# One query copy on ScalarE in place of GpSimd, and the low parts of the weights in two halves

## The chip, the cores and the metric

The kernel runs on one core of a Trainium2 chip. The metric is the device time of one execution in microseconds (us). The core has five engines, each with its own queue of instructions that it takes in order: TensorE (PE, with its weight loads as PEld), VectorE (DVE), ScalarE (ACT), GpSimd (POOL) and SyncE (SP), which issues most of the DMAs. An engine waits on semaphores for what other engines and DMAs have done.

## The reference

Two things are computed one after the other. First an attention over 8 batches, 8 heads, 576 positions and 64 values per head, in which a query sees only a window of keys: the last 32 for heads 0 to 3, every fourth of the last 128 for heads 4 to 7.

```
scores = scale * np.matmul(q, k.transpose(0, 1, 3, 2))
scores = np.where(masks, scores, -1e9)
attn = softmax(scores)
x = np.matmul(attn, v)        # then heads side by side: x is 8 x 576 x 512
```

Then in each batch the 128 rows with the highest score `x @ w_gate` go through two matrices (512x1024 and 1024x512) with a ReLU between them, and are added back, weighted with the sigmoid of their score:

```
scores = np.einsum('bsd,d->bs', x, w_gate)
top_idx = np.argpartition(-scores[b], capacity)[:capacity]
h = np.maximum(x[b, top_idx] @ w1, 0.0)
out[b, top_idx] = x[b, top_idx] + g[:, None] * (h @ w2)
```

## The kernel before, in words

The order of all work is written out by hand in one text, ORDER (lines 44 to 112). Each entry names a step and its batch, and a loop at the end of the kernel calls the step's function; since every engine takes its instructions in order, this text sets the order on each engine. The steps that matter here, as `NAME batch part`:

- Q and K load transposed queries and keys with SyncE's DMAs (lines 290 to 303). For each batch there are two kinds of heads (kind 0: the plain window, kind 1: every fourth key).
- ZP, ZV and ZA are the same function, `spread` (line 306): it copies one half of the loaded queries (64 partitions, h = 0 or 1) into a padded tile `zq` whose other places hold zeros. ZP does so on GpSimd, ZV on VectorE, ZA on ScalarE. There is one `zq` tile for each kind, so it is written anew in every batch once the last scores that read it are done.
- S (line 352 on) makes the scores of one of five groups of a batch: two matmuls with the masks, then 24 or 32 small matmuls of `kq` and `zq` into a PSUM tile `s` (line 363). There are two `s` tiles.
- MX takes the maxima on VectorE (line 370). Then either CS copies the scores to SBUF on ScalarE (line 377) and SP2 subtracts the maxima on GpSimd (line 382), or SU subtracts on VectorE. TR transposes the differences (line 389), EX takes the exponentials on ScalarE (lines 398 and 402), V multiplies with the values (line 417), DN and XM divide on VectorE (lines 426 to 438), ST stores the rows to HBM with SyncE's DMAs (lines 448 to 456).
- GD multiplies the rows with the gate and sums them, two instructions of VectorE with two inputs in SBUF, `x` and `wg` (line 474; the tile `warm` takes the product, which nobody needs). RX/RP, RO, SC, SP and RK make scores and ranks out of the sums (`gs`, then `ts`), and W fills TensorE's time with matmuls that read `warm` (line 712).
- GT gathers the chosen rows with an indirect DMA of GpSimd (line 597), XT transposes them (line 632), XH and XL split them into a high and a low part (lines 635 and 638). F and N are the first matrix (lines 653 and 669), Y is the second (line 694), YO the sum (line 699), SY the indirect store back (line 704), again from GpSimd.

The two matrices are held as a high part in a rounded format and a low part, what is left. LW loads one of eight blocks of 128x1024 as `raw` (lines 605 and 607; there are two `raw` tiles), WH rounds it on ScalarE (line 617), WL subtracts on GpSimd (line 621). The blocks are loaded and split between the attention steps of batches 0 to 4, and each product is then three matmuls: high by high, high by low, low by high.

Around the change in ORDER (lines 74 to 76) stand, in this order: GT 2 and SY 0 on GpSimd; ZV 4 0 0 on VectorE; CS 3 2 on ScalarE; the copy of the other half, ZP 4 0 1; the scores S 4 4 and S 4 3, the first to read `zq` of batch 4; EX 4 0, XH 1 and EX 3 3 on ScalarE; SP2 3 2 on GpSimd; then TR 3 2, XT 2, V 3 3 and S 4 2 on TensorE, and the first matrix of the next group (F 1 ..).

Of the kernel before, what the change touches and what calls it, by code (L numbers as in the profile page):

```python
# [8 lines left out]
F32 = mybir.dt.float32  # L9
# [4 lines left out]
ALU = mybir.AluOpType  # L14
# [3 lines left out]
B, H, S, D = 8, 8, 576, 64  # L18
DM, FF = 512, 1024
# [52 lines left out]
GD 2 2, SC 2, SP 2, ST 2 3, MX 3 4, V 3 0, VL 3 1, SU 3 4, ZP 4 1 0, ST 2 4, GT 1, RK 2 0, EX 3 1, RK 2 1, RK 2 2,  # L72
RK 2 3, TP 2, Q 4 0, S 4 1, RK 2 4, S 4 0, SP2 3 3, TR 3 3, WH 7, DN 3 0, K 4 0, MX 4 1, WL 7, RC 2, RA 2, TR 3 4,
MV 2, Y 0 6, CS 4 1, SP2 4 1, Y 0 7, MX 4 0, XA 3 0, PK 2, S 3 2, IX 2, GT 2, V 3 1, DT 4 0, SU 4 0, YO 0, Q 5 0,
TR 4 0, TR 4 1, DN 3 1, EX 3 4, XM 3 1, SY 0, ZV 4 0 0, XT 1, V 3 4, MX 3 2, DN 3 4, CS 3 2, ZP 4 0 1, S 4 4, S 4 3,
XM 3 4, EX 4 0, VL 5 2, XH 1, SP2 3 2, EX 3 3, TR 3 2, XT 2, ST 3 4, XL 1, V 3 3, CS 4 4, MX 4 4, XH 2, S 4 2, XL 2,
F 1 1 0, F 1 0 0, F 1 1 1, F 1 0 1, GM 3 0, GA 3 0, DT 4 3, MX 4 3, SU 4 3, F 1 0 2, SP2 4 4, GD 3 4, SG 2, DN 3 3,
EX 3 2, F 1 2 0, SG 1, F 1 1 2, F 1 1 3, GD 3 1, ST 3 1, RX 3, SH 1, ST 3 0, MX 4 2, XM 3 3, ZP 5 0 1, EX 4 1,
# [37 lines left out]
def tile_window_attention_moe(ctx, tc, qt, kt, va, vb, w_gate, w1, w2, masks, mask_l, ident, slots, toks, outs, capacity):  # L116
    nc = tc.nc
# [55 lines left out]
    X = {}  # L173
# [132 lines left out]
    def spread(copy, b, kind, h, part=None):  # L306
        r, src = slice(HB * h, HB * (h + 1)), qs[b, kind]
        n = 16 if kind else 18
        lo, hi = (0, n) if part is None else (0, 8) if part == 0 else (8, n)
        copy(zqs[kind][r, :, lo:hi, h], src[r, :, G * lo:G * hi].rearrange("p g (t q) -> p g t q", q=G))  # L310
        if hi == n:
            if kind:
                copy(zqs[kind][r, :, n:n + 4, h, 0:16], src[r, :, 4 * P:S].rearrange("p g (t q) -> p g t q", q=16))
            over(("q", b, kind), src, 2)
# [64 lines left out]
    def subtract(eng, b, u):  # L379
        st, mx = X.pop(("s", b, u)), X.pop(("mx", b, u))  # L380
        dt = X["dt", b, u]
        eng.tensor_tensor(out=dt, in0=st if eng is nc.vector else dt, in1=mx.unsqueeze(2).to_broadcast([P, 8, GK]), op=ALU.subtract)  # L382
# [46 lines left out]
    def divide(b, u, on_act):  # L429
        av, rin = heads(X.pop(("a", b, u))), X.pop(("rin", b, u))  # L430
        X["x", b, u] = x = xs.pop(0)
        xv = x.rearrange("p e (i d) -> p e i d", i=4)
        if on_act:
            for e in range(2):
                for i in range(4):
                    nc.scalar.activation(xv[:, e, i], av[:, e, i, 0:D], AF.Copy, scale=rin[:, e, i:i + 1])
        else:
            nc.vector.tensor_tensor(out=xv, in0=av[:, :, :, 0:D], in1=rin.unsqueeze(3).to_broadcast([P, 2, 4, D]), op=ALU.mult)  # L438
# [171 lines left out]
    def weight_parts(i):  # L610
        if i < 4:
            return (w[:, i] for w in (w1h, w1l))
        return (w[:, 2 * i - 8:2 * i - 6].rearrange("k j f -> k (j f)") for w in (w2h, w2l))
# [4 lines left out]

    def weights_low(i):
        hi, lo = weight_parts(i)  # L620
        nc.gpsimd.tensor_tensor(out=lo, in0=X.pop(("raw", i)), in1=hi.bitcast(F32), op=ALU.subtract)

    TERMS = (("h", "h", 0), ("h", "l", 1), ("l", "h", 2))
    WS1, WS2 = dict(h=w1h, l=w1l), dict(h=w2h, l=w2l)
# [83 lines left out]
    def idle(n):  # L708
# [8 lines left out]
        ZA=lambda *i: spread(nc.scalar.copy, *i), VL=load_v, C=constants, W=idle, S=scores, MX=maximum, SU=lambda *i: subtract(nc.vector, *i), DT=differences, CS=copy_scores, SP2=lambda *i: subtract(nc.gpsimd, *i), TR=turn, EX=exps,  # L717
        V=attend, DN=divisors, XM=lambda b, u: divide(b, u, False), XA=lambda b, u: divide(b, u, True), ST=store,
        GM=gate_mult, GA=lambda b, u: gate_sum(b, u, False), GD=lambda b, u: gate_sum(b, u, True),
        RX=lambda b: split_sums(nc.vector, b), RP=lambda b: split_sums(nc.gpsimd, b), TP=score_parts, RO=in_order, SC=total_score, SP=as_row, RK=rank, RC=rank_others, RA=rank_total,  # L720
        MK=lambda b: mark(b, 0, nc.gpsimd), MV=lambda b: mark(b, 0, nc.vector), PK=pick, IX=index, SG=sig_exp, SH=sig,
        GT=gather, LW=load_weights, WH=lambda i: weights_high(i, nc.scalar.copy), WV=lambda i: weights_high(i, nc.vector.tensor_copy),
        WL=weights_low, YO=result, SY=scatter)
    groups = {}
    for name in ORDER.split("\n"):
# [120 lines left out]
```

## Time and profile before

| what | us |
|---|---|
| median of 3 runs | 263.73 |
| lowest and highest of them | 262.48, 264.22 |
| the profiled execution | 263.13 |
| its span in the trace | 261.4 |
| TensorE busy in the span | 233.8 |
| VectorE, GpSimd, ScalarE busy | 183.2, 127.2, 121.0 |

The rows further down come from the one profiled execution, with times counted from the start of its span. A row of a timeline has the start, the duration, the engine, the line of the kernel, the operation, what is written and read, and how many instructions of it are merged; in brackets the time that the engine stood idle before it and what ended that. A name such as `zq L310` is the tile and the line of the instruction that wrote it. A granted clock of 1.00 is 2.4 GHz, one of 0.50 is 1.2 GHz.

### The profile page before, as it was taken

How to read it: one execution, taken by the hardware profiler on the slowest of the kernel's cores; microseconds unless marked ns; L12 is line 12 of the kernel's file. 1: busy time of each engine (PE TensorE's matmuls, PEld its weight loads, DVE VectorE, ACT ScalarE, POOL GpSimd, SP SyncE). 2: the span in 40 equal slices, each digit the busy share in tenths (PEclk: the TensorE clock that was granted, in tenths of full speed). 3: DMA queues.
4: the chain of work that ended last, by engine and by line, in shares of the span. 5: the costliest groups of instructions: out<-in, count | busy, mean ns of one | idle time of the engine just before them, and what ended most of it. 6: DMA issues, size and time to landing. Idle time of an engine off the chain costs nothing.

```text
span 261.4 us, 8703 instructions
## 1 busy us (share of the span) xinstructions
PE 233.8 (89%) x3560; PEld 205.1 (78%) x3560; DVE 183.2 (70%) x540; ACT 121.0 (46%) x265; POOL 127.2 (49%) x192
## 2 busy tenths in 40 slices
PE   5897689976998893899999988999999999999991
PEld 3785588875896682799888977999898888988880
DVE  6676998869789985185678687787878688831231
ACT  5278457693468445161613455863560443101120
POOL 6199769778578743612413658331427434110111
PEclk9799979997999998599999999999999999999999
DMA  6999797969749597907593753499258322201102
GB/s 239 391 374 326 219 380 252 330 203 332 299 146 337 180 332 233 286 4 234 206 301 143 239 181 112 115 289 386 98 146 290 97 80 95 94 0 40 43 0 80
DMA packets 22712, 53.14 MB, mean 203 GB/s; under 512 B 2816, under 2 KB 13440, under 8 KB 21648
## 3 DMA queue, kind: packets, MB, share of 16 engines
q1 hardware_dynamic: 20496, 47.63, 53.5%
q0 software_dynamic: 1344, 4.26, 5.0%
q10 hardware_dynamic: 832, 0.69, 0.8%
q8 instruction: 28, 0.46, 0.7%
q14 instruction: 12, 0.10, 0.1%
HBM read 41.04 MB, written 11.53 MB: 201 GB/s over the span
## 4 chain that ended last, share of the span: by engine, by line
PE 66%; DVE 18%; DMA 5%; ACT 4%; POOL 3%; issue 3%; POOLq 1%; SPq 0%; DVEq 0%; ACTq 0%
PE m L653 14%; PE m L694 14%; PE a L417 11%; PE s L363 10%; DVE warm L474 7%; PE m L669 5%; PE m L389 4%; PE s L356 3%; DVE x L438 2%; ACT pt L402 2%; DVE mx L370 2%; PE m L523 2%; DMA mraw<-in_masks_dram 2%; DMA out_dram<-x 1%; DMA out_dram<-y,ix 1%
## 5 line engine op out<-in xcount | busy, mean ns | idle before, releaser
L363 PEld LDWEIGHTS s<-kq,zq 128*64 128x64 f32 x1216 | 45.4, 148 | 9.9 <-POOL zq L310 5.8
L363 PE MATMUL s<-kq,zq 128*64 128x64 f32 (+2 forms) x1216 | 46.0, 232 | 6.1 <-POOL zq L310 5.2
L417 PE MATMUL a<-v,pt 128*64 128x65 f32 x1152 | 46.5, 226 | 3.5 <-DVE x L438 3.3
L417 PEld LDWEIGHTS a<-v,pt 128*64 128x64 f32 x1152 | 41.7, 140 | 8.4 <-issue 3.4
L382 POOL TENSOR_TENSOR dt<-dt,mx 128x512 f32<-128x512 f32 x28 | 29.9, 1070 | 33.6 <-DVE mx L370 19.1
L474 DVE CUSTOM_DVE_ANT_0 warm<-x,wg 128x256 bf16<-128x256 f32 x68 | 41.5, 610 | 4.3 <-PE m L712 2.6
L377 ACT COPY dt<-s 128x512 f32<-128x512 f32 x28 | 16.4, 587 | 49.0 <-DVE mx L370 21.5
L402 ACT ACTIVATE pt<-m 64x512 f32<-64x512 f32 x48 | 28.4, 591 | 14.4 <-PE a L417 5.6
L370 DVE TENSOR_REDUCE mx<-s 128x8 f32<-128x512 f32 x40 | 27.0, 680 | 11.4 <-ACT dt L377 8.9
L398 ACT ACTIVATE pt<-m 32x256 f32<-32x256 f32 (+1 forms) x80 | 30.1, 376 | 8.1 <-PE m L389 6.9
L310 POOL COPY zq<-kq 64x1152 f32<-64x1152 f32 (+1 forms) x21 | 24.4, 1161 | 16.3 <-PE s L363 5.4
L653 PE MATMUL m<-xh,w1h 128*128 128x256 f32 x96 | 28.3, 295 | 0.0
L694 PE MATMUL m<-w2h,hh 128*128 128x512 f32 x64 | 27.3, 427 | 0.0
L653 PE MATMUL m<-xl,w1h 128*128 128x256 f32 x96 | 27.0, 282 | 0.0
L653 PE MATMUL m<-xh,w1l 128*128 128x256 f32 x96 | 26.9, 280 | 0.0
L438 DVE TENSOR_TENSOR x<-a,rin 128x512 f32<-128x512 f32 x37 | 25.5, 690 | 1.6 <-DVE rin L427 0.2
L389 PE MATMUL m<-id,dt 128*128 128x128 f32 x160 | 25.2, 283 | 0.9 <-POOL dt L382 0.5
L694 PE MATMUL m<-w2l,hh 128*128 128x512 f32 x64 | 25.3, 395 | 0.0
L694 PE MATMUL m<-w2h,hl 128*128 128x512 f32 x64 | 25.2, 394 | 0.0
L530 DVE SCALAR_TENSOR_TENSOR rm<-m,ts,thr 128x512 bf16<-128x512 f32 (+3 forms) x40 | 21.3, 584 | 1.9 <-PE m L523 1.9
L658 ACT ACTIVATE hh<-m 128x512 fp32r<-128x512 f32 x12 | 7.0, 599 | 31.8 <-PE m L653 21.6
L389 PEld LDWEIGHTS m<-id,dt 128*128 128x128 f32 x160 | 18.1, 142 | 4.0 <-POOL dt L382 1.0
(125 smaller groups left out, 430.1 us busy)
## 6 DMA issues: line engine op xcount, KB each, us to landing
v<-in_va_dram SPq DMA_DIRECT2D x8, 1170.0 KB, 9.0
kq<-in_qt_dram SPq DMA_DIRECT2D x15, 576.0 KB, 6.3
kq<-in_kt_dram SPq DMA_DIRECT2D x15, 576.0 KB, 6.3
out_dram<-x SPq DMA_DIRECT2D x32, 256.0 KB, 4.0
v<-in_va_dram SPq DMA_DIRECT2D x8, 520.0 KB, 5.1
raw<-in_w_dram SPq DMA_DIRECT2D x8, 512.0 KB, 5.7
vl<-in_vb_dram SPq DMA_DIRECT2D x16, 97.5 KB, 5.0
kq<-in_kt_dram SPq DMA_DIRECT2D x2, 288.0 KB, 7.5
```

The costliest lines, as they stand in the source:

```text
L310: copy(zqs[kind][r, :, lo:hi, h], src[r, :, G * lo:G * hi].rearrange("p g (t q) -> p g t q", q=G))
L363: nc.tensor.matmul(st[HB * g:HB * (g + 1), i, lo:hi], zqs[kind][:, g, t].rearrange("p h q -> p (h q)"), ks[b, kind][:, g, k0 + lo:k0 + hi] ...
L370: nc.vector.tensor_reduce(out=mx, in_=X["s", b, u], axis=AX.X, op=ALU.max)
L382: eng.tensor_tensor(out=dt, in0=st if eng is nc.vector else dt, in1=mx.unsqueeze(2).to_broadcast([P, 8, GK]), op=ALU.subtract)
L389: nc.tensor.transpose(tt[:, a * P:(a + 1) * P], dt[:, 2 * a:2 * a + 2].rearrange("p e k -> p (e k)"), id32)
L398: nc.scalar.activation(pt[o:o + n, y, e], tt[lo:lo + n, x].rearrange("k c (i q) -> k c i q", q=G), AF.Exp, scale=SCALE)
L402: nc.scalar.activation(pt[r, :, e], tt[r].rearrange("k (i q) -> k i q", q=G), AF.Exp, scale=SCALE)
L417: nc.tensor.matmul(av[r, a // 2, f], pt[:, i % 2, i // 2, a], values(b, u, a)[:, f], start=True, stop=True)
L438: nc.vector.tensor_tensor(out=xv, in0=av[:, :, :, 0:D], in1=rin.unsqueeze(3).to_broadcast([P, 2, 4, D]), op=ALU.mult)
L474: nc.vector.tensor_tensor_reduce(out=warm, in0=X["x", b, u][:, c], in1=gate_w(u)[:, c], scale=UP, scalar=0.0, op0=ALU.mult, op1=ALU.add, a ...
L653: nc.tensor.matmul(out, WS1[w][:, i, f * P:(f + 1) * P], X["x" + x, e][:, i, :], start=i == 0 and n == 0, stop=i == 3 and n == 2)
L694: nc.tensor.matmul(X["py", b], X["h" + x, e, c][:, o:o + P], WS2[w][:, i, :], start=i == 0 and k == 0, stop=i == 7 and k == 2)
```

## The change

Two edits. In ORDER the entry ZP 4 0 1 becomes ZA 4 0 1, at the same place: the copy of half 1 of batch 4's kind-0 queries is an instruction of ScalarE's queue, behind CS 3 2, and no longer one of GpSimd's. In `weights_low` the subtraction of a block is written as two instructions of 512 columns each, in place of one of 1024, for all eight blocks; what is computed is the same.

```
-XM 3 1, EX 3 4, ... CS 3 2, ZP 4 0 1, S 4 4, S 4 3,
+XM 3 1, EX 3 4, ... CS 3 2, ZA 4 0 1, S 4 4, S 4 3,
...
     def weights_low(i):
         hi, lo = weight_parts(i)
-        nc.gpsimd.tensor_tensor(out=lo, in0=X.pop(("raw", i)), in1=hi.bitcast(F32), op=ALU.subtract)
+        raw = X.pop(("raw", i))
+        for h in range(2):
+            f = slice(h * FF // 2, (h + 1) * FF // 2)
+            nc.gpsimd.tensor_tensor(out=lo[:, f], in0=raw[:, f], in1=hi[:, f].bitcast(F32), op=ALU.subtract)
```

## Rows read from the trace of the kernel before

**Rows 1.** The page's part 1: busy us, share, instructions of TensorE.
```profile
PE 233.8 (89%) x3560; PEld 205.1 (78%) x3560; DVE 183.2 (70%) x540; ACT 121.0 (46%) x265; POOL 127.2 (49%) x192
```
**Rows 2.** Waits of TensorE: line and whom it waited for; us, times, longest.
```profile
PE s L363 <- POOL zq L310: 5.2, 1, 5.2
PE a L417 <- DVE x L438: 3.3, 4, 1.7
PE m L523 <- DVE ts L509: 3.2, 2, 2.0
PE m L712 <- DVE gs L474: 2.2, 1, 2.2
```
**Rows 3.** Stretches: length, busy us of each engine, granted clock, DMA share, GB/s.
```profile
35.00:38.40 3.40, 3.40 (x68) 3.40 (x64) 3.26 (x10) 2.19 (x5) 2.17 (x3) 0.50 1.03 415
...
59.00:62.30 3.30, 1.30 (x24) 1.08 (x21) 3.13 (x6) 1.33 (x4) 3.18 (x4) 1.00 1.00 266
62.30:65.70 3.40, 3.40 (x9) 2.63 (x9) 3.37 (x13) 0.59 (x1) 2.16 (x3) 0.50 1.00 412
...
103.20:110.10 6.90, 4.48 (x63) 4.18 (x64) 1.39 (x2) 2.13 (x4) 4.45 (x4) 0.51 0.78 230
110.10:150.00 39.90, 39.90 (x583) 35.89 (x582) 28.94 (x90) 16.41 (x41) 13.46 (x22) 1.00 0.56 191
```
**Rows 4.** Timeline of TensorE: S 4 4 and V 3 3.
```profile
105.62 1.52 PE L363 MATMUL s<-kq,zq 128*64 128x64 f32 x24 [5.16 <-POOL zq L310]
...
110.62 1.15 PE L417 MATMUL a<-v,pt 128*64 128x65 f32 x32
```
**Rows 5.** Timeline of GpSimd: SY 0, ZP 4 0 1, SP2 3 2.
```profile
100.34 1.02 POOL L704 DMA_INDIRECT out_dram<-y,ix  x1 [0.30 <-issue]
104.43 1.14 POOL L310 COPY zq<-kq 64x1152 f32<-64x1152 f32 x1 [3.07 <-DMA out_dram<-y,ix]
105.65 1.04 POOL L382 TENSOR_TENSOR dt<-dt,mx 128x512 f32<-128x512 f32 x1
```
**Rows 6.** Line 310 on GpSimd, 97 to 107: semaphore waits (ns; first and last start).
```profile
L310 POOLq EVENT_SEMAPHORE  x3: 17/43/43, 103.5 to 104.3; - x3
```
**Rows 7.** Timeline of VectorE: ZV 4 0 0.
```profile
99.16 0.75 DVE L310 COPY zq<-kq 64x1152 f32<-64x1152 f32 x1 [0.27 <-DMA kq<-in_qt_dram]
```
**Rows 8.** Groups of ScalarE by form: busy us, mean ns, idle before.
```profile
L310 ACT COPY zq<-kq 64x1152 f32<-64x1152 f32 x2 | 2.3, 1142 | 0.0
```
**Rows 9.** Timeline of ScalarE: CS 3 2, EX 4 0, EX 3 3.
```profile
100.60 0.59 ACT L377 COPY dt<-s 128x512 f32<-128x512 f32 x1 [3.79 <-DVE den L426]
101.08 1.98 ACT L398 ACTIVATE pt<-m 64x256 f32<-64x256 f32 x5
103.08 0.59 ACT L635 CAST xh<-m 128x512 fp32r<-128x512 f32 x1
103.56 1.21 ACT L402 ACTIVATE pt<-m 64x512 f32<-64x512 f32 x2
```
**Rows 10.** Groups of GpSimd by form: busy us, mean ns, idle before.
```profile
L382 POOL TENSOR_TENSOR dt<-dt,mx 128x512 f32<-128x512 f32 x28 | 29.9, 1070 | 33.6 <-DVE mx L370 19.1 <-ACT dt L377 14.0
...
L310 POOL COPY zq<-kq 64x1024 f32<-64x1024 f32 x10 | 10.9, 1087 | 0.2
...
L466 POOL TENSOR_TENSOR gm<-x,wg 128x512 f32<-128x512 f32 x6 | 7.7, 1284 | 13.9 <-DVE x L438 12.5 <-DVE g L589 1.4
```
**Rows 11.** Timeline of VectorE: products and sums of line 474.
```profile
57.92 0.43 DVE L474 CUSTOM_DVE_ANT_0 warm<-x,wg 128x256 bf16<-128x256 f32 x1
...
58.39 2.56 DVE L474 CUSTOM_DVE_ANT_0 warm<-x,wg 128x256 bf16<-128x256 f32 x1
...
78.77 2.53 DVE L474 CUSTOM_DVE_ANT_0 warm<-x,wg 128x256 bf16<-128x256 f32 x1
```
**Rows 12.** Timeline of GpSimd: a copy behind a weight subtraction, and one such subtraction.
```profile
33.08 1.23 POOL L310 COPY zq<-kq 64x1024 f32<-64x1024 f32 x1
...
58.32 2.36 POOL L621 TENSOR_TENSOR w1l<-raw,w1h 128x1024 fp32r<-128x1024 f32 x1 [0.30 <-ACT w1h L617]
```

More of the change, by code (lines that the diff above doesn't have):

```diff
@@ L74 @@
 MV 2, Y 0 6, CS 4 1, SP2 4 1, Y 0 7, MX 4 0, XA 3 0, PK 2, S 3 2, IX 2, GT 2, V 3 1, DT 4 0, SU 4 0, YO 0, Q 5 0,
-TR 4 0, TR 4 1, DN 3 1, EX 3 4, XM 3 1, SY 0, ZV 4 0 0, XT 1, V 3 4, MX 3 2, DN 3 4, CS 3 2, ZP 4 0 1, S 4 4, S 4 3,
+TR 4 0, TR 4 1, DN 3 1, EX 3 4, XM 3 1, SY 0, ZV 4 0 0, XT 1, V 3 4, MX 3 2, DN 3 4, CS 3 2, ZA 4 0 1, S 4 4, S 4 3,
 XM 3 4, EX 4 0, VL 5 2, XH 1, SP2 3 2, EX 3 3, TR 3 2, XT 2, ST 3 4, XL 1, V 3 3, CS 4 4, MX 4 4, XH 2, S 4 2, XL 2,
```

## The prediction

> **What bounds the kernel now.** I read the page first: TensorE is busy for 89% of the span, far ahead of the other engines [rows 1]. Then the waits of TensorE alone, longest first: they are few, and one of them, 5.2 us for a copy of queries that GpSimd makes, is the longest; behind it stand 3.3 us for VectorE's `x`, 3.2 us for `ts` and 2.2 us for `gs` [rows 2]. Then the table by stretches: from 110.1 to 150.0 TensorE is busy for all 39.90 us of it at full clock, and after the first 12 us three stretches before 110.1 ran at a granted clock of about 0.5, that is 1.2 GHz in place of 2.4 [rows 3]. So TensorE's work is the bound, and what can be won lies before 110: its waits, and the stretches at 1.2 GHz that follow the waits of 2.2, 2.0 and 5.16 us. A us that TensorE wins there is still won at the end if the engines that feed it come along; VectorE, ScalarE and GpSimd all have room after 110.
>
> At the great gap the reader is to see four things. The matmuls of S 4 4 stand 5.16 us for `zq` and start at 105.62, at half clock [rows 4]. GpSimd issues the indirect store at 100.34 and is done with it at 101.36, but the copy (ZP 4 0 1) starts at 104.43, and the end of its wait is put down to the landing of that store, not to the load of the queries [rows 5]. Three semaphore waits stand before that copy, from 103.5 to 104.3 [rows 6]. And VectorE's copy of the other half (ZV 4 0 0), out of the same load, starts at 99.16: the queries were there long before [rows 7].
>
> **The copy, ZP 4 0 1 to ZA 4 0 1.** Removed: 1.14 us of GpSimd behind the store. Added: one copy of the same form on ScalarE, 1.14 us there too [rows 8]. In ScalarE's queue it stands behind the score copy CS 3 2 (100.60, 0.59 us) and ahead of five exponentials (1.98 us), `xh` (0.59) and two more exponentials (1.21 us from 103.56) [rows 9]. So it runs from about 101.1 to 102.25, and S 4 4 can start at 102.3 in place of 105.62: 3.3 us. I assume that no wait for the store goes with it, because the copy of the other half had none [rows 7].
>
> What is late next? Before, S 4 4 to the start of V 3 3 took 110.62 - 105.62 = 5.0 us at half clock [rows 4], which is 2.5 us at full. V 3 3 needs the two exponentials that now end 1.14 us later, at 103.56 + 1.21 + 1.14 = 105.9 [rows 9]; that is the earliest. The idle time before S 4 4 is 1.8 us now. Waits of 2.0 and 2.2 us were each followed by one stretch of 3.4 us at 1.2 GHz, the wait of 5.16 us by 6.9 us of it [rows 2 to 4]. If the clock falls for 3.4 us some 0.9 us after the start, V 3 3 starts at 102.3 + 0.9 + 2 x 1.6 = 106.4; if it does not fall, at 105.95; if it stays low all the way, at 102.3 + 5.0 = 107.3. So TensorE wins 3.3 to 4.7 us here; I take 4.2, the middle case. The next step on GpSimd, the subtraction SP2 3 2, waited behind the copy and started at 105.65 [rows 5]; it can now follow ScalarE's score copy at about 101.4, in time for its transposes. Behind ScalarE's copy the exponentials and `xh` come 1.14 us later than before counted from 101.08, and their reader V 3 3 has over 4 us of room in the old order: hidden, and worth at most that 1.14 us if the room were gone. No DMA is moved.
>
> **The halves.** Eight subtractions of 128x1024 become sixteen of 128x512. First their own price. The whole one takes 2.36 us [rows 12]; the nearest rows of half the width are a subtraction at 1.07 and a product at 1.28 us [rows 10]. A pair is then between 2 x 1.07 = 2.14 and 2 x 1.28 = 2.56 us: -0.2 to +0.2 for each of eight. I take +0.05, since the subtraction is the same operation and the product another, so 0.4 us of GpSimd in all, of which perhaps 0.3 us lies where GpSimd works without a pause.
>
> The Trainium skill, GPSIMD Engine Reference, § 3.1, speaks against halves: each instruction is said to pay two software hops and a join of eight cores, and a two-input add of 2048 columns takes 4497 ns. As an estimate, a line through that figure and the row of this trace for 1024 columns has a fixed part of about 0.23 us, so each pair would be 0.23 us dearer, 1.9 us over eight if none of it were hidden. The row of the 512-wide subtraction is below half of the whole one and bears out no such part; no row here has this subtraction itself at 512.
>
> What they buy is on VectorE. The product-and-sum of line 474 reads two SBUF tensors; alone it takes 0.43 us, but at 58.39 it took 2.56 and at 78.77 2.53 [rows 11]. At 58.32 GpSimd had begun a whole weight subtraction, which ran to 60.68; VectorE's instruction ended at 60.95, 0.27 us later [rows 11, 12]. So it stood until GpSimd's instruction was over. There are four such holds behind weight subtractions (two more, at 30.98 and 83.24). Who goes first when GpSimd's next instruction is ready too? At 33.08 GpSimd's next copy took 1.23 against a mean of 1.09 of its form, so VectorE was let in between two instructions of GpSimd [rows 10, 12]. A hold that begins early in the subtraction should thus end one half, 1.1 us, sooner, and the second half waits some 0.3 us for it.
>
> - Hold at 58.39: TensorE waits 2.0 us for `ts` behind it [rows 2]. With 1.1 us less it waits 0.9. From 62.3 to 65.7 it was then busy 3.40 us at half clock [rows 3], work of 1.7 us at full. Another wait of 1.7 us (the longest for `x` [rows 2]) had no such stretch behind it, so I expect none behind 0.9. Together 2.8 us for TensorE; VectorE itself wins only its 1.1 and must deliver later in the same batch, so I take 2.4. Bounds: 0 and 2.0 + 1.7 = 3.7.
> - Hold at 78.77: 1.1 us sooner, and the wait for `x` that follows is 1.0 us long; the hold at 83.24 is followed by the other wait for `ts`, 3.2 - 2.0 = 1.2 us [rows 2]. The two overlap on VectorE; I take 1.0. Bounds: 0 and 2.2.
> - Hold at 30.98: TensorE waits 2.2 us for `gs` and then works 3.40 us at half clock [rows 2, 3]. But VectorE's next products are of the same kind and meet the second half, so its own chain wins little. I take 0.7. Bounds: 0 and 1.1.
> - The other four subtractions hold nobody: nothing.
>
> **The sum**, against the profiled execution of 263.13 us (a span of 261.4 and 1.7 around it): -4.2 - 2.4 - 1.0 - 0.7 + 0.3 = -8.0, so 255.1. The median of the three runs is 0.6 us above the profiled one: 255.7 us.
>
> **The rivals.**
> - Only the copy pays. VectorE's products come in pairs; if the first is let in after one half and the second is held by the other, the pair ends when it did, and GpSimd has only grown. For it: the port passes back and forth, as at 33.08 [rows 12]. Against it: behind the hold at 58.39 comes no second product. Time: 263.73 - 4.2 + 0.4 = 259.9.
> - Transfers bound the part before 100. The DMA share is 1.00 from 59.0 to 65.7 [rows 3], and VectorE's copy at 99.16 waited for the load of the queries [rows 7]. If that load does not come sooner, all that is won before is given back at 99, and the copy's 4.2 remain: 259.5. Against it: the load is issued in SyncE's queue behind stores that wait for VectorE, so it moves along.
> - The change does not do what it says: the wait for the store belongs to the data and goes to ScalarE with the copy. Then S 4 4 starts at 105.6 as before, and the halves alone give 263.73 - 3.8 = 259.9. Against it: rows 7, and that ScalarE's two copies of this very form show no idle time before them [rows 8].
> - Slower: the halves make GpSimd the bound. Place: the stretches before 100 in which GpSimd goes from one instruction to the next. If a half costs as much as the product, 1.28, and lets VectorE in each time for some 0.2, a pair is 2.96 against 2.36, 0.6 dearer, 4.8 over eight; with the least gain of the copy, 3.3, and nothing from the holds: 263.73 + 4.8 - 3.3 = 265.2. It decides once a half costs more than about 1.4 us and VectorE wins nothing.
>
> **How the numbers follow.** The forecast, 255.7, has a chance of 0.53; its own range from the bounds is 252 to 259. Only the copy 0.20, transfers 0.11, not what it says 0.07, slower 0.04, and 0.05 for no change by a wait that I do not see. The low end: 4.7 + 3.7 + 2.2 + 1.1 = 11.7 less than 263.73, about 252.0. The high end takes in the three rivals near 260 with a us of scatter: 261.0. A measurement can tell about 1%, 2.6 us, from no change. Faster by more than that, under 261.1: 0.53 + 0.20 + 0.11 + 0.07 less a little = 0.89. Within 1%: the unseen wait and most of the slower case, 0.08. Slower: 0.03.
>
> **What would show it.** Right: TensorE's wait before S 4 4 is under 2 us; ScalarE has a 1.14 us copy about 0.1 us behind CS 3 2; SP2 3 2 starts before ScalarE's copy ends; no product of line 474 is longer than about 1.7 us behind a weight subtraction; a half takes 1.05 to 1.3 us; no stretch at 1.2 GHz near 62. Wrong: three semaphore waits ahead of ScalarE's copy that end with the store's landing; holds that come in twos and add up to the old length; new waits of TensorE for loaded tensors before 100; or a span that shrinks before 110 and grows again behind it.

## The result, and the profile after

Six runs of the changed kernel have a median of 254.0 us (251.9 to 254.6); six of the kernel before, on the same chip, 262.59 (260.76 to 264.22). The ratio is 0.9714, with a 95% interval of 0.967 to 0.9758: faster by 2.9%, or 7.5 us. The ratios here and below are the measurement's own estimates with their intervals; they are not the quotients of the medians shown, which would be 0.967 here. The forecast of 255.7 against 263.73 was a ratio of 0.970. The profiled execution took 253.94 us, its span is 252.2, so 9.2 us less than the span before.

The page of the kernel after, parts 1 and 2: busy time of the engines, and TensorE's granted clock in 40 slices.

```profile
PE 230.0 (91%) x3560; PEld 200.8 (80%) x3560; DVE 182.3 (72%) x540; ACT 122.1 (48%) x266; POOL 128.3 (51%) x199
...
PEclk9999999999999999999999999999999999999997
```

TensorE is busier by share and in sum still the bound [rows 1]. Its clock shows no slice below 9 ahead of the last one; before, three stretches ran at about 0.5 [rows 3]. That is one execution: in e9, a second profile of the same kernel, the clock was 0.50 from 39.6 to 43.0. VectorE's busy time fell by 0.9 us only, GpSimd's grew by 1.1, although a copy of 1.14 us left it.

The waits of TensorE in the kernel after (line, whom it waited for; us in total, times, longest). The new lines of code moved 712 to 715 and 632 to 635.

```profile
PE m L523 <- DVE ts L509: 2.4, 2, 1.4
PE a L417 <- DVE x L438: 2.2, 3, 1.7
PE s L363 <- ACT zq L310: 1.9, 2, 1.6
...
PE m L715 <- DVE gs L474: 1.1, 1, 1.1
...
PE m L635 <- ACT pt L402: 1.0, 1, 1.0
```

Against [rows 2]: the wait for the query copy went from 5.2 to 1.6 us, now behind ScalarE. `gs` went from 2.2 to 1.1, the longest wait for `ts` from 2.0 to 1.4, `x` from 3.3 to 2.2. One wait is new, 1.0 us of line 635 for ScalarE's exponentials.

The gap itself, first ScalarE's timeline after, then TensorE's, then GpSimd's (start, us, engine, line, operation; in brackets the idle time before and what ended it).

```profile
95.35 0.58 ACT L377 COPY dt<-s 128x512 f32<-128x512 f32 x1 [3.44 <-DVE mx L370]
95.96 1.15 ACT L310 COPY zq<-kq 64x1152 f32<-64x1152 f32 x1
97.13 1.98 ACT L398 ACTIVATE pt<-m 64x256 f32<-64x256 f32 x5
99.13 0.59 ACT L638 CAST xh<-m 128x512 fp32r<-128x512 f32 x1
99.61 1.21 ACT L402 ACTIVATE pt<-m 64x512 f32<-64x512 f32 x2
```

```profile
97.16 0.91 PE L363 MATMUL s<-kq,zq 128*64 128x64 f32 x24 [1.58 <-ACT zq L310]
...
100.88 0.66 PE L635 MATMUL m<-id,xe 128*128 128x128 f32 x4 [0.99 <-ACT pt L402]
101.46 1.15 PE L417 MATMUL a<-v,pt 128*64 128x65 f32 x32
```

```profile
95.09 1.02 POOL L707 DMA_INDIRECT out_dram<-y,ix  x1 [0.30 <-issue]
96.14 1.05 POOL L382 TENSOR_TENSOR dt<-dt,mx 128x512 f32<-128x512 f32 x1
```

ScalarE's copy stands 0.03 us behind the score copy and waits for no store. The scores S 4 4 start 1.58 us after TensorE's last work, at full clock (24 matmuls in 0.91 us; before, 1.52 [rows 4]). GpSimd's subtraction runs straight behind the store instead of 5.3 us after its issue [rows 5]. S 4 4 began 8.46 us sooner than before and V 3 3 (line 417) 9.16 us; the span shrank by 9.2. So nothing of it was given back in the 150 us behind.

The hold of line 474 that stood at 58.39 before, on VectorE after:

```profile
57.12 1.37 DVE L474 CUSTOM_DVE_ANT_0 warm<-x,wg 128x256 bf16<-128x256 f32 x1
```

The third and fourth of four weight halves in a row on GpSimd at that time, merged into one line, and then an undisturbed pair:

```profile
56.79 2.83 POOL L624 TENSOR_TENSOR w1l<-raw,w1h 128x512 fp32r<-128x512 f32 x2
...
67.73 2.51 POOL L624 TENSOR_TENSOR w2l<-raw,w2h 128x512 fp32r<-128x512 f32 x2
```

The third half, taken alone, is 1.42 us long and ends at 58.21. VectorE's instruction ends at 58.49, 0.28 us later: it was let in between two instructions of GpSimd, and the pair paid for it with 2.83 in place of 2.51. The undisturbed pair takes 0.15 us more than one whole subtraction [rows 12].

### The profile page after: what moved, and what is told of

It is laid out like the page before. It is cut to its first block, busy times and chain, and to the rows that moved or that the text cites. A ratio compares the mean times of both kernels' runs of the same rounds, so it can differ in the third digit from the quotient of the medians.

```text
span 252.2 us, 8710 instructions
## 1 busy us (share of the span) xinstructions
PE 230.0 (91%) x3560; PEld 200.8 (80%) x3560; DVE 182.3 (72%) x540; ACT 122.1 (48%) x266; POOL 128.3 (51%) x199
## 4 chain that ended last, share of the span: by engine, by line
PE 65%; DVE 16%; ACT 8%; DMA 4%; issue 3%; SPq 2%; POOLq 0%; POOL 0%; DVEq 0%; ACTq 0%
PE m L656 14%; PE m L697 14%; PE a L417 11%; PE s L363 8%; DVE warm L474 5%; PE m L672 4%; PE m L389 4%; ACT pt L402 3%; DMA kq<-in_kt_dram 2%; DVE x L438 2%; PE s L356 2%; ACT dt L377 2%; PE m L523 2%; DMA mraw<-in_masks_dram 2%; DVE mx L370 2%
## 5 line engine op out<-in xcount | busy, mean ns | idle before, releaser
L363 PEld LDWEIGHTS s<-kq,zq 128*64 128x64 f32 x1216 | 42.7, 141 | 6.2 <-ACT zq L310 2.5
L417 PEld LDWEIGHTS a<-v,pt 128*64 128x64 f32 x1152 | 41.0, 138 | 7.7 <-issue 4.1
L363 PE MATMUL s<-kq,zq 128*64 128x64 f32 (+2 forms) x1216 | 43.4, 225 | 2.2 <-ACT zq L310 1.9
L474 DVE CUSTOM_DVE_ANT_0 warm<-x,wg 128x256 bf16<-128x256 f32 x68 | 40.9, 602 | 4.0 <-PE m L715 2.3
L310 POOL COPY zq<-kq 64x1152 f32<-64x1152 f32 (+1 forms) x20 | 22.2, 1110 | 9.6 <-PE s L363 6.0
```

Of the source, the lines that this page charges most:

```text
L363: nc.tensor.matmul(st[HB * g:HB * (g + 1), i, lo:hi], zqs[kind][:, g, t].rearrange("p h q -> p (h q)"), ks[b, kind][:, g, k0 + lo:k0 + hi] ...
L417: nc.tensor.matmul(av[r, a // 2, f], pt[:, i % 2, i // 2, a], values(b, u, a)[:, f], start=True, stop=True)
L474: nc.vector.tensor_tensor_reduce(out=warm, in0=X["x", b, u][:, c], in1=gate_w(u)[:, c], scale=UP, scalar=0.0, op0=ALU.mult, op1=ALU.add, a ...
```

## The experiments

Each was timed beside the kernel before on the same chip; the ratio is to those runs, with its 95% interval. A row per kernel:

| kernel | median us (lowest to highest, runs) | ratio, interval |
|---|---|---|
| e1 copy on ScalarE alone | 257.44 (256.06 to 259.1, 4) | 0.9829, 0.9754 to 0.9904 |
| e2 halves alone | 258.82 (256.89 to 260.99, 10) | 0.9884, 0.9837 to 0.993 |
| e3 copy, halves in blocks 1, 3, 5, 6 | 254.03 (253.77 to 255.05, 4) | 0.9689, 0.9633 to 0.9745 |
| e4 copy, halves in blocks 0, 2, 4, 7 | 257.3 (255.61 to 260.22, 4) | 0.9806, 0.9713 to 0.9899 |
| e5 the two copies exchanged | 258.19 (255.34 to 258.72, 4) | 0.9784, 0.9682 to 0.9886 |
| e6 the store behind the copy | 262.57 (259.75 to 264.44, 8) | 0.9955, 0.9893 to 1.0017 |
| e7 as e3, in quarters | 256.86 (253.2 to 259.07, 4) | 0.9789, 0.9695 to 0.9882 |
| e8 exchange, halves as e3 | 253.57 (252.59 to 253.84, 4) | 0.9625, 0.9542 to 0.9707 |
| e9 the changed kernel again | 254.67 (254.42 to 255.42, 6) | 0.9676, 0.9636 to 0.9716 |
| e10 as e3, again | 254.32 (253.69 to 254.58, 6) | 0.9653, 0.9613 to 0.9693 |
| e11 as e8, again | 253.67 (252.58 to 255.51, 6) | 0.9645, 0.9598 to 0.9692 |

**e1: the copy alone.**

```
-CS 3 2, ZP 4 0 1, S 4 4,
+CS 3 2, ZA 4 0 1, S 4 4,
```

> Only the query copy goes to ScalarE; the weight subtractions stay whole. My theory: the two edits add up, and this one alone is worth the 4.2 us that TensorE won between the S 3 2 matmuls and the first matrix in the changed kernel: ratio 0.984, about 258.4 us where the kernel before has 262.6; the three long holds of line 474 (2.4 to 2.6 us) stay, and so does a stretch at 1.2 GHz behind each. Rival (the edits need each other): without the halves the wait before S 4 4 still ends in a fall of the clock, and only 3.3 us or less are won, ratio 0.988 or more.

Measured: 1.7% faster, about 4.5 us. The ratio is near the theory's, but its interval takes in the rival's 0.988 too; the trace decides between them. TensorE's timeline of e1 at the gap:

```profile
99.89 0.91 PE L363 MATMUL s<-kq,zq 128*64 128x64 f32 x24 [1.58 <-ACT zq L310]
...
103.61 0.66 PE L632 MATMUL m<-id,xe 128*128 128x128 f32 x4 [0.99 <-ACT pt L402]
104.19 1.15 PE L417 MATMUL a<-v,pt 128*64 128x65 f32 x32
```

Its two waits are those of the changed kernel to the hundredth. From TensorE's last work before the gap to V 3 3 it is 1.58 + 4.30 = 5.88 us, against 5.16 + 5.00 = 10.16 before [rows 4]: 4.28 us won, in this kernel and in the changed one alike. The expected stretch at 1.2 GHz near 62 did not come, although the long holds stayed (see the clock, below).

**e2: the halves alone.**

```
-        nc.gpsimd.tensor_tensor(out=lo, in0=X.pop(("raw", i)), in1=hi.bitcast(F32), op=ALU.subtract)
+        raw = X.pop(("raw", i))
+        for h in range(2):
+            f = slice(h * FF // 2, (h + 1) * FF // 2)
+            nc.gpsimd.tensor_tensor(out=lo[:, f], in0=raw[:, f], in1=hi[:, f].bitcast(F32), op=ALU.subtract)
```

> Only the halves; the copy stays on GpSimd behind the indirect store. My theory: the holds behind weight subtractions end one half sooner, TensorE's waits before 60 shrink and no stretch near 62 runs at 1.2 GHz, while the wait of 5.2 us for zq stays: 4.9 us won, ratio 0.981, about 257.7 us. Rival (only the copy pays): ratio 1.000.

Measured: 1.2% faster, about 3.0 us. The theory's 4.9 us (0.981) and the rival's 1.000 both lie outside the interval: the halves pay, but less than expected (4.9 is what the copy's 4.28 leaves of the 9.2 us between the two profiled executions). The wait of 5.1 us at the gap is still there:

```profile
PE s L363 <- POOL zq L310: 5.1, 1, 5.1
PE m L523 <- DVE ts L509: 2.4, 2, 1.4
```

The two edits add up within the noise: 0.9829 x 0.9884 = 0.9715, and 0.9714 was measured for both together. That they agree to 0.0001 is chance; the intervals are wider by far.

**e3 and e4: which halves.** Both have the copy on ScalarE; the subtraction is in two pieces for four of the eight blocks and whole for the others. In e3 they are the four behind which a long hold stood, in e4 the other four.

```
+        n = 2 if i in (1, 3, 5, 6) else 1
...
```

```
+        n = 1 if i in (1, 3, 5, 6) else 2
...
```

The loop that is cut here then makes n pieces of each block.

> As the changed kernel, but only blocks 1, 3, 5 and 6, behind which a product of line 474 was held, are subtracted in halves; blocks 0, 2, 4 and 7 whole. My theory: the gain of the halves is all in these four; the other four only pay 0.2 us each for the second instruction, little of it on the path: 0 to 0.6 us faster than the changed kernel, ratio to the kernel before 0.969 to 0.971. Rival (shorter instructions help GpSimd's queue everywhere): slower than the changed kernel, ratio 0.975 or more.

> As the changed kernel, but with halves only for blocks 0, 2, 4 and 7, whose subtraction held no product of line 474; blocks 1, 3, 5 and 6 whole. My theory: nothing of the halves' gain is left, the time is that of the kernel with the copy alone or up to 0.6 us above it: ratio 0.984 to 0.987. Rival (shorter instructions help everywhere): half of the halves' gain, ratio about 0.977.

Measured: e3 gives all that the change gives. e4's ratio, 0.9806, lies between its theory and its rival, and its interval holds both as well as the copy's 0.9829, so e4 alone does not decide; but no run of e3 is above 255.05 and none of e4 below 255.61. All products of line 474 in e3, then in e4 (minimum, median and longest in ns):

```profile
L474 DVE CUSTOM_DVE_ANT_0 warm<-x,wg x68: 373/425/1489, 24.1 to 213.8; 128x256 bf16<-128x256 f32 x68
```

```profile
L474 DVE CUSTOM_DVE_ANT_0 warm<-x,wg x68: 375/425/2490, 23.4 to 215.2; 128x256 bf16<-128x256 f32 x68
```

A product is still held for 2.49 us in e4 and none for more than 1.49 in e3. So the gain of the halves lies in the holds that they cut; that the halves of the other four blocks add nothing that can be measured is borne out by e3 and e10, which do without them.

**e5 and e6: what the copy waited for.** In e5 VectorE takes half 1 and GpSimd half 0, still behind the store. In e6 GpSimd keeps half 1, and the store's issue is put behind it.

```
-XM 3 1, SY 0, ZV 4 0 0, XT 1, ... CS 3 2, ZP 4 0 1, S 4 4,
+XM 3 1, SY 0, ZV 4 0 1, XT 1, ... CS 3 2, ZP 4 0 0, S 4 4,
```

```
-XM 3 1, SY 0, ZV 4 0 0, XT 1, ... CS 3 2, ZP 4 0 1, S 4 4,
+XM 3 1, ZV 4 0 0, XT 1, ... CS 3 2, ZP 4 0 1, SY 0, S 4 4,
```

> The kernel before, weight subtractions whole, with the two halves of the copy exchanged: VectorE takes half 1 (partitions 64 to 127) where it took half 0, and GpSimd takes half 0, still behind the indirect store; ScalarE takes none. My theory: the wait for the indirect DMAs belongs to GpSimd's copies of half 1 alone (in the kernel before, a copy of half 0 started at 151.67, right behind a gather issued at 150.62, while the copy of half 1 behind it stood until 156.28). Then GpSimd's copy starts at about 101.4, the wait of 5.2 us shrinks to about 2, ratio 0.984. Rival: any copy of GpSimd behind an indirect store waits for its landing: the wait of 5 us stays, ratio 1.000.

> The kernel before with one entry moved: the indirect store SY 0 stands behind ZP 4 0 1 instead of ahead of it. My theory: GpSimd's copy waits for every indirect DMA of GpSimd that is under way, so also for the gather GT 2 (the first of its three waits was met at 103.5, the store's at 104.2): the copy starts about 0.7 us sooner and TensorE's wait is still over 4 us; ratio 0.995 to 1.000. Rival (it waits for the store alone): the copy starts right behind the gather, TensorE's wait is about 2 us, ratio 0.984.

Measured: e5 is as fast as e1, e6 as slow as before within its interval. GpSimd's timeline of e5, then of e6:

```profile
98.38 1.23 POOL L597 DMA_INDIRECT xe<-out_dram,ix  x1 [3.01 <-DVE rin L427]
99.91 1.02 POOL L704 DMA_INDIRECT out_dram<-y,ix  x1 [0.30 <-issue]
100.94 1.15 POOL L310 COPY zq<-kq 64x1152 f32<-64x1152 f32 x1
```

```profile
95.59 0.98 POOL L597 DMA_INDIRECT xe<-out_dram,ix  x1 [2.26 <-DMA kq<-in_qt_dram]
102.31 1.14 POOL L310 COPY zq<-kq 64x1152 f32<-64x1152 f32 x1 [5.74 <-DMA out_dram<-x]
103.74 1.04 POOL L704 DMA_INDIRECT out_dram<-y,ix  x1 [0.29 <-POOL zq L310]
```

In e5 the copy of half 0 on GpSimd starts the moment that the store's issue is over, with a gather and a store under way. In e6 no store is ahead of the copy of half 1, and it still stands 5.74 us, with 5.3 us for TensorE before S 4 4. Two semaphore waits lie before it (line 310 on GpSimd in e6, from 97 to 107), and the list of DMA issues from 94 to 104 has the gather (the last number is the us from issue to landing):

```profile
L310 POOLq EVENT_SEMAPHORE  x2: 42/42/43, 102.1 to 102.2; - x2
```

```profile
xe<-out_dram,ix POOLq DMA_INDIRECT x1, 6.5
```

The gather, issued at 95.59, lands 6.5 us later at 102.1, where the two waits end. Before there were three waits, from 103.5 to 104.3 [rows 6]; with the store moved away one is gone. The DMA issues before, from 98 to 106, have the gather (issued at 98.68) and the store (at 100.34):

```profile
xe<-out_dram,ix POOLq DMA_INDIRECT x1, 4.8
out_dram<-y,ix POOLq DMA_INDIRECT x1, 3.9
```

They land at 103.5 and 104.2, where the first wait and the second end, and the trace's records of these waits name the semaphores that the gather and the store set. So GpSimd's copy of half 1 (partitions 64 to 127) waits for every indirect DMA of GpSimd that is under way, the gather as well as the store; the DMA that the timeline of e6 names, `out_dram<-x`, is another that landed at that time. The waits are instructions of the program. In the changed kernel the same three stand from 102.2 to 102.4 before GpSimd's next copy of a half 1, and both DMAs have landed by then (5.5 and 4.5 us after their issues at about 93.4 and 95.09). The two query copies of later batches in the kernel before agree:

```profile
150.62 1.05 POOL L597 DMA_INDIRECT xe<-out_dram,ix  x1 [0.70 <-issue]
151.67 1.05 POOL L310 COPY zq<-kq 64x1024 f32<-64x1024 f32 x1
...
156.28 2.83 POOL L310 COPY zq<-kq 64x1152 f32<-64x1152 f32 x2 [2.33 <-DMA xe<-out_dram,ix]
```

The copy at 151.67, a half 0, stands right behind the gather; the copies from 156.28 on, led by a half 1, waited for it. Why the waits are put on one half and not on the other was not tried.

**e7: finer still.** The held blocks in four pieces of 256 columns.

```
+        n = 4 if i in (1, 3, 5, 6) else 1
...
```

> As the changed kernel, but blocks 1, 3, 5 and 6 in four pieces of 256 columns and the others whole. My theory: a hold ends after one quarter (0.7 us) in place of one half (1.3), 0.6 us sooner, but each piece costs about 0.2 us more and lets VectorE in again for 0.2: what VectorE wins GpSimd gives back; within 1 us of the kernel with these four in halves, ratio 0.966 to 0.973. Rival (the finer the better): half of what the halves gave once more, ratio 0.961 or less.

Measured: four runs from 253.2 to 259.07, at a ratio 1.0% above that of e3; 0.9789 is above what the theory said and far above the rival's 0.961. Its GpSimd rows by form:

```profile
L625 POOL TENSOR_TENSOR w1l<-raw,w1h 128x256 fp32r<-128x256 f32 x8 | 6.6, 850 | 0.1
L625 POOL TENSOR_TENSOR w1l<-raw,w1h 128x1024 fp32r<-128x1024 f32 x2 | 4.9, 2466 | 0.0
```

Two blocks in quarters cost GpSimd 6.6 us where two whole ones cost 4.9. The profiled execution, with a span of 251.5, has two waits for `gs` of at most 0.6 us; the other runs are slower and unprofiled, so why they spread stays open. One product in it is held for 2.38 us, and not by a weight subtraction. VectorE, then GpSimd:

```profile
34.72 2.38 DVE L474 CUSTOM_DVE_ANT_0 warm<-x,wg 128x256 bf16<-128x256 f32 x1
```

```profile
34.27 1.31 POOL L310 COPY zq<-kq 64x1024 f32<-64x1024 f32 x1
35.52 0.29 POOL L313 COPY zq<-kq 64x128 f32<-64x128 f32 x1
35.78 1.04 POOL L382 TENSOR_TENSOR dt<-dt,mx 128x512 f32<-128x512 f32 x1
```

It stood through the rest of one GpSimd instruction and two more: that VectorE is let in between two instructions of GpSimd is what most holds here show, not a rule. No gain of finer cuts is shown; that they are worse is not shown either, since the intervals of e3 and e7 overlap.

**e8 to e11: a better version?** e8 and e11 have the exchange of e5 and the halves of e3. It is meant to spare TensorE the new wait of 1.0 us behind ScalarE's exponentials.

```
-XM 3 1, SY 0, ZV 4 0 0, XT 1, ... CS 3 2, ZP 4 0 1, S 4 4,
+XM 3 1, SY 0, ZV 4 0 1, XT 1, ... CS 3 2, ZP 4 0 0, S 4 4,
...
+        n = 2 if i in (1, 3, 5, 6) else 1
...
```

> The exchange of the two halves of the copy (VectorE half 1, GpSimd half 0, ScalarE none) with blocks 1, 3, 5 and 6 in halves and the others whole. My theory: in the changed kernel TensorE waits 0.99 us at line 635 for the exponentials that ScalarE's copy pushed back; without that copy on ScalarE this wait goes, and the other wait, before S 4 4, stays near 1.6 us: about 1 us faster than the kernel with ScalarE's copy and the same halves, ratio 0.965. Rival (another wait ends there as late): no difference from it, ratio 0.969. If GpSimd's copy waits for the store after all: ratio 0.985.

> The changed kernel once more, beside the two variants of the same call. Theory (copy 1.7%, held halves 1.2%, halves of the other four blocks worth nothing): ratio 0.971 to the kernel before, as measured. Rival (the four halves that nothing needs cost TensorE time): over 0.5% above e10.

> ScalarE's copy and halves for blocks 1, 3, 5 and 6 alone. Theory: the same as e9 within 0.4%, since the other four blocks' halves lie beside TensorE's work. Rival: faster than e9 by 0.5% or more, GpSimd being about 1 us less busy.

> The two copies of the queries exchanged between GpSimd and VectorE instead of one given to ScalarE, halves for blocks 1, 3, 5 and 6. Theory: TensorE no longer waits 1.0 us for a PSUM bank that ScalarE's evictions free, and loses nothing elsewhere: 0.4% faster than e10 (about 1 us), ratio 0.965. Rival (e8's lead was the chip's): the same ratio as e10 within 0.2%.

Measured: e9, e10 and e11 ran beside one another. e10 is 0.35 us (0.14%) under e9: the four halves that nothing needs cost less than can be told. e11 is 0.65 us (0.26%) under e10 and 1.0 us under e9, between what theory and rival said; by the ratios it is 0.1% under e10, the rival's case, and all three intervals overlap. In e11 TensorE's wait for `pt` ahead of the transposes is 0.29 us in place of 0.99, and the copy's is 1.5 us:

```profile
PE s L363 <- POOL zq L310: 1.5, 1, 1.5
```

From TensorE's last work before the gap to V 3 3 e11 takes 1.55 + 3.51 = 5.06 us, against 5.88 with ScalarE's copy. e8's ratio lies 0.6% under e3's, e11's 0.1% under e10's; the gap is shorter by 0.8 us, but that the exchange makes the whole kernel faster than the changed one is not shown.

## Why the prediction was right

The forecast's sum was 8.0 us less than the profiled execution before; the profiled execution after is 9.2 us less, the medians of the same chip differ by 8.6, and the ratio gives 7.5. Both mechanisms held, the wait that stays with GpSimd and the holds that end a half sooner. But up to the gap e1 runs the kernel before's own instructions, and its profiled execution ends its last work there at 98.31, where the one before ended it at 100.46: 2.15 us of the lead are a difference between executions. The rest is the change: 100.46 - 95.58 = 4.88 us of lead at the gap in the kernel after, so 2.73 us against e1 for the halves, and 4.28 for the copy. The three make 9.16, the lead at V 3 3. By its steps:

**The copy, 4.2 us.** The assumption that no wait for the store goes with it held. The wait before S 4 4 was taken at 1.8 us and is 1.58. From S 4 4 to V 3 3 the middle case (a fall of the clock 0.9 us after the start) gave 4.1 us; it is 4.30, in another way. The clock did not fall. Instead the transposes of line 635 wait 0.99 us for a PSUM bank that ScalarE's exponentials (99.61 + 1.21 = 100.82) have to read first, and V 3 3 comes behind those transposes. The prediction had seen that the exponentials come 1.15 us later and had named V 3 3 as their reader, but put the limit at 3.65 us after the start of S 4 4. It left out that the 0.6 us of transposes stand between. Together 4.28 us, and 4.5 by e1's ratio.

**The holds, 4.1 us less 0.3.** VectorE was let in between the halves, as [rows 10, 12] had suggested: no product is longer than 1.45 us now. "VectorE's own chain wins little" was right in general: all 68 products of line 474 took 41.5 us before and 40.9 after.

```profile
L474 DVE CUSTOM_DVE_ANT_0 warm<-x,wg 128x256 bf16<-128x256 f32 x68 | 40.9, 602 | 4.0 <-PE m L715 2.3
```

That is 0.6 us in sum, because a second product in a row now meets the second half. TensorE won more than that, since it waits for single products: the hold that ended last became 1.2 us shorter, and VectorE lost the time again later, where nobody waited for it.

- At 58.39, 2.4 us. TensorE's wait for `ts` there went from 2.00 to 1.06, 0.94 where 1.1 had been taken. The rest was to come from the clock: from the first to the tenth matmul behind the wait it is 65.87 - 62.11 = 3.76 us before and 2.21 after, 1.55 less. But in e1, with the hold whole, it is 2.20: this share is not shown to be the halves' (see the clock), and the term is over-sized without it.
- At 78.77 and 83.24, 1.0 us less some price: from 66 us to the gap TensorE's lead grew from 4.0 to 4.88 us, 0.9.
- At 30.98, 0.7 us. The wait for `gs` fell by 1.1, and at the wait for `ts` the lead was 59.51 - 58.00 = 1.51 us, where e1, without halves, had 0.60 at the same place. So 0.9: a little under-sized.

Against e1 that is 0.94 + 0.9 + 0.9, the 2.73 us above, and near the 3.0 us of e2's ratio; the sum had 3.8 for the halves.

**The price of a half, 0.3 us in all, was mis-sized.** The row taken, a subtraction with 1.07 us, was the wrong neighbour. The subtractions of the kernel after:

```profile
L624 POOL TENSOR_TENSOR w1l<-raw,w1h 128x512 fp32r<-128x512 f32 x8 | 10.9, 1385 | 0.0
L624 POOL TENSOR_TENSOR w2l<-raw,w2h 128x512 fp32r<-128x512 f32 x8 | 10.5, 1327 | 1.1 <-ACT w2h L617 1.1
```

and of the kernel before:

```profile
L621 POOL TENSOR_TENSOR w1l<-raw,w1h 128x1024 fp32r<-128x1024 f32 x4 | 9.6, 2409 | 0.3 <-ACT w1h L617 0.3
L621 POOL TENSOR_TENSOR w2l<-raw,w2h 128x1024 fp32r<-128x1024 f32 x4 | 9.5, 2374 | 2.5 <-PE m L680 1.4 <-ACT w2h L617 1.1
```

They cost GpSimd 21.4 us in place of 19.1: 2.3 more, not 0.4. An undisturbed half takes 1.27 us, near the product (1.284 [rows 10]); eight pairs at 0.15 are 1.2 us, and the rest is what the halves pay when they let VectorE in. It cost TensorE little: e10 has half as many halves and is 0.14% faster than e9, too little to tell from no difference. The slower rival needed a half dearer than 1.4 us and nothing won from the holds; the longest are 1.48, but the holds paid.

The Trainium skill, GPSIMD Engine Reference, § 3.1, was weighed in the prediction: by an estimate from its figure a pair should cost 0.23 us more than the whole (0.22, and 1.8 over eight, when the line is redone). The undisturbed pair shows 0.15, so its warning of a fixed part was right where the row chosen against it was not.

**The clock.** The prediction gave the halves a share of the 1.7 us that the stretch at 1.2 GHz behind the wait of 2.0 us for `ts` had cost. e1 shows that the wait alone doesn't bring that stretch. Its wait, then its stretch behind it and an earlier one (length, busy us of PE, PEld, DVE, ACT, POOL, granted clock, DMA share, GB/s):

```profile
PE m L523 <- DVE ts L509: 3.1, 2, 2.0
```

```profile
62.30:65.70 3.40, 3.40 (x16) 2.78 (x15) 3.37 (x16) 0.42 (x1) 1.55 (x3) 1.00 1.03 420
32.70:36.10 3.40, 3.40 (x60) 3.17 (x58) 2.89 (x10) 0.59 (x1) 1.13 (x3) 0.50 0.99 380
```

With the same wait of 2.0 us the clock stayed at 1.00 in e1. In e5, whose wait is the same too, it fell as before:

```profile
PE m L523 <- DVE ts L509: 3.1, 2, 2.0
```

```profile
62.00:65.40 3.40, 3.40 (x11) 2.76 (x10) 3.37 (x13) 0.58 (x1) 2.31 (x3) 0.56 1.04 427
```

And e2, whose wait for `gs` is only 1.1 us, ran at 0.50 from 32.4 to 35.8. The pages of e1 and of e2 by slices:

```profile
PEclk9999979999999999999999999999999999999997
```

```profile
PEclk9799979999999998899999999999999999999998
```

So a part of what the profile of before offered was luck of that execution, and "no stretch at 1.2 GHz near 62" was no sure sign of the halves. Over all thirteen profiles the stretch near 62 stands in two (before, e5) of the five whose held blocks are whole and in none of the eight where they are cut; a stretch that begins between 32 and 40 stands in eight, with and without cuts (e9 has it, e4 has none). Behind the gap the picture is clear: the clock fell in the three whose wait there was over 5 us (before, e2, e6) and in none of the ten with 1.9 us or less. Over many runs the direction still holds: the mean granted clock was 0.968 over the 37 runs of the kernel before beside these experiments, 0.984 in e1, 0.981 in e2, 0.989 in the changed kernel; and among the 37 runs a straight line gives 1.25 us less for each 0.01 of clock (correlation -0.75). By that line some 1.5 of e2's 3.0 us and 2.0 of e1's 4.5 go along with the clock. That is a relation between runs, worked out from their clocks, not an experiment on the clock.

**The rivals.** "Only the copy pays" falls with e2 and e3; "transfers bound the part before 100" with the lead of 4.88 us that TensorE kept up to the gap; "does not do what it says" with ScalarE's copy above. The forecast held, but part of its closeness is luck: it gave the halves 1.7 us of the clock that another execution has without them, and the one pair of profiles then showed 2.15 us more than the change is worth by e1.

## What to carry to other kernels

When one engine's long instruction holds another's short one, cut the long one only where something late waits behind the hold: here four of the eight cuts gave all of the gain, and no gain of cuts finer than a half could be shown. When an instruction waits for a DMA whose data it doesn't touch, try the same instruction on the next engine or with the next half: e1 and e5 both made the wait go. And before a stretch at the low clock is booked as a gain, look whether it stands in a second profile.

## What was not expected of the hardware

GpSimd's copies of partitions 64 to 127 waited for all its indirect DMAs under way, 5.74 us in e6 with no store ahead; its copies of partitions 0 to 63 of the same form did not (e5: at once behind the issue), nor did VectorE's and ScalarE's. These waits are instructions of the program, so the runs show where they stand, not that the chip needs them. VectorE's two-input product was mostly let in between two GpSimd instructions (1.45 us at most after, 2.56 before), but in e7 it stood 2.38 us through parts of three. And the clock differs between runs of one order of work: a wait of 2.0 us was followed by 3.4 us at 1.2 GHz in the profile before [rows 3], and by none in e1; e5, with the same wait, fell again.
